# Two interleaved layers of Hedgehog attention and a squared-ReLU MLP: turned blocks' transfers tied behind the weight loads, and low parts of turned features on GpSimd

## The chip, the cores and the metric

The kernel runs on one core of one Trainium2 chip. The metric is the device time of one execution in microseconds (us). The engines are TensorE (PE; its weight loads are listed as PEld), VectorE (DVE), ScalarE (ACT), GpSimd (POOL) and SyncE (SP), which issues nearly all DMAs here.

## The reference

Two layers; in each, an attention with a learned feature map is added to x, then an MLP with squared ReLU. S = 2048 rows, D = 576, H = 32 heads of 18, F = 4608, all fp32.

```python
def attention(x):                       # of a layer-normed x
    q, k, v = split_heads(x @ wqkv)
    pq, pk = q @ w_phi, k @ w_phi       # per head, 18x18
    phi_q = concat(softmax(pq), softmax(-pq))
    phi_k = concat(softmax(pk), softmax(-pk))
    kv, z = phi_k.T @ v, sum(phi_k)
    return (phi_q @ kv) / (phi_q @ z + 1e-6) @ wo
def mlp(x):
    return relu(x @ w1 + b1) ** 2 @ w2 + b2
for layer in range(2):
    x = x + attention(layernorm(x))
    x = x + mlp(layernorm(x))
```

## The kernel before

**Tiles.** The 2048 rows are four blocks of 512, each four tiles of 128. fp32 operands are split into a high part, rounded to the matmul's format, and a low part that holds the rest; each product is three matmuls: high by high, high by low, low by high. ACT makes a high part (a copy), DVE or POOL the low part (a subtraction).

**Stages.** A layer has an attention block that nothing covers (t0, t1), and then four MLPs, one for each block, of which two run as a pair. The first two MLPs of each layer are woven with attention of other blocks: m_3 (layer 0) and m_1 (layer 1) with the output of block a_2 (a_0) and the queries and features of a_0 (a_3); m_2 and m_0 with the output of a_0 (a_3) and then all of a_1 (a_2). In the names of the order the layer stands first: `m0_2` is m_2 in layer 0, `a0_1` is a_1 in layer 0; the trace leaves it out.

**An MLP step.** There are 36 steps, each for 128 columns of F. Step f loads w1's and w2's parts (`r1`, `r2`, lines 1159 and 1161, on SP), splits them (`h1`, `s2`: ACT at lines 1167 to 1169, the low parts on DVE at 1171 and 1174 and on POOL at 1175), makes `ph` in 14 matmuls (L1190), applies relu on ACT (`hr`, L1197), makes the high part `hb` on ACT (L1198), squares on ACT (L1199) and leaves the low part to DVE (L1200), and adds to `acc` in 15 matmuls (L1217 and L1208). As a rule `ph` of step f+1 stands between `ph` and `acc` of step f, so that ACT and DVE have the time of 14 matmuls.

**The turned features.** `g_features` makes the features of a block's four tiles: exponentials, sums, factors, scale (L853 and its neighbours), then `turn`: DVE transposes blocks of 32x32 in place (L897), and SP writes the tile in four DMAs into a DRAM buffer `ft` (L900). `g_out` reads them back feature by row (`fetch`, L928) in five groups of 126 or 72 partitions: two fetches are asked for at its start, the others as the groups are used. For each half of a group ACT makes the high part `fh` (L941) and DVE the low part `fl` (L942), and PE multiplies them with the keys' sums (`pn`, L964, three matmuls for each of ten half groups). ACT and DVE split the result `pn` (L966 to L970), and it is multiplied with wo (`po`, L999), added to x, and normed. The group tiles share four buffers (tag E) with the exponentials; `fh` and `fl` share four (tag ft).

**What sets the order.** The program is written as Python generators. `weave(main, other, rate)` interleaves the steps of an MLP with those of attention by the costs that the steps yield; `pipeline` runs stages over tiles one behind the other, the costs being the numbers in its last argument. A list scheduler then fixes the order in which each engine's instructions stand, with its own estimates of their costs, and the order is static on the chip: an instruction that waits holds up all behind it on its engine. `tc.issue_after(ins)` ties what is traced inside it behind `ins`; `held` ties the steps of a generator behind the last instructions of the MLP's step that `dense` remembers; `traced_on(engine)` is the instruction that the program traced last for an engine. DMAs on SP wait at SP's head for what they read or overwrite, so that a load behind a transfer waits for that transfer's source.

Of the kernel before, what the change touches and what calls it, by code (L numbers as in the profile page):

```python
# [13 lines left out]
P = 128  # L14
TB = 512
NT = TB // P
# [5 lines left out]
def layers_kernel(  # L22
# [96 lines left out]
    def pipeline(n, stages, costs):  # L119

        for i in range(n + len(stages) - 1):
            for k in reversed(range(len(stages))):
                if 0 <= i - k < n:
                    stages[k](i - k)
                    yield costs[k]
# [9 lines left out]
    def traced_on(engine):  # L135
        return next(i for i in reversed(nc.cur_bb.bb.instructions) if i.engine == engine.engine)
# [519 lines left out]
    def soft_exp(e):  # L656
        return nc.scalar.activation(e, e, AF.Exp)
# [148 lines left out]
    def held(gen, keys=("last",)):  # L806

        while True:
            with ExitStack() as behind:
                for key in keys:  # L810
                    behind.enter_context(tc.issue_after(dense[key].ins))
                cost = next(gen, gen)
            if cost is gen:
                return
            yield cost
# [63 lines left out]
    def g_features(layer, raws, ph, name):  # L879

        rs, ms = {}, {}

        def start(t):
            ph.append(soft_parts(raws[t], f"{name}Q{t}"))

        def add(t):
            rs[t] = soft_sums(ph[t], f"{name}Q{t}")
            ms[t] = phi_products(layer, ph[t], f"{name}m{t}")

        def factors(t):  # L890
            phi_factors(phi_sums(ms.pop(t), f"{name}u{t}"), rs[t])

        turned[name] = home = dram.tile([2 * D, TB], F32, name=f"{name}ft")

        def turn(t):
            flat = ph[t].rearrange("p s d -> p (s d)")
            nc.vector.transpose(flat, flat)  # L897
            for i in range(NQ):
                at = t * P + 32 * i
                nc.sync.dma_start(home[:, at : at + 32].rearrange("(j f) r -> f j r", f=32),  # L900
                                  flat[32 * i : 32 * i + 32].rearrange("f (j r) -> f j r", r=32))

        yield from held(pipeline(NT, (start, lambda t: soft_exp(ph[t]), add, factors, lambda t: phi_scale(ph[t], rs[t]),
                                      turn), (2.6, 0.4, 3.0, 2.8, 1.2, 1.6)), ("last", "squared"))

    def g_out(layer, b, ph, dst, name, parts=1, pause=None, behind=None, norm=None, mid=None, costs=(None, None), o_first=None):

# [14 lines left out]
        def fetch(k):  # L922
            if k < NG:
                g, w = groups[k], gw[groups[k]]
                raws[g] = sb.tile([P, 2 * D], F32, tag="E", name=f"{name}w{g}", bufs=4)[:w, : 2 * TB]
                raws[g] = raws[g].rearrange("p (s n) -> p s n", s=2)
                src = turned[name].rearrange("(s d) n -> d s n", s=2)
                nc.sync.dma_start(raws[g], src[g * GW : g * GW + w])  # L928

        def turn(part, i):  # L930
            g, s = groups[i // 2], i % 2
            w = gw[g]
            new = lambda k: sb.tile([GW, TB], F32R, tag="ft", name=f"{name}f{k}{g}{s}{part}", bufs=4)[:w]
            if parts > 1:
                f = new("")
                fh, fl = (f[:, k * pw : (k + 1) * pw] for k in range(2))
            else:
                if s == 0:
                    fetch(i // 2 + 2)
                fh, fl = (new(k) for k in "hl")  # L940
                dense["turn", i] = nc.scalar.activation(fh, raws[g][:, s], AF.Copy)  # L941
                dense["turned"] = nc.vector.tensor_sub(fl, raws[g][:, s], fh.bitcast(F32))  # L942
                return fh, fl
            pt = wtile(f"{name}pt{g}{s}{part}")
            for t in range(NT // parts):
                nc.tensor.transpose(pt[:w, t * P : (t + 1) * P],
                                    ph[part * NT // parts + t][:, s, g * GW : g * GW + w], ident)
            dense["turn", i] = nc.scalar.activation(fh, pt[:w, :pw], AF.Copy)
            dense["turned"] = nc.vector.tensor_sub(fl, pt[:w, :pw], fh.bitcast(F32))
            return fh, fl  # L950
# [62 lines left out]
        if parts == 1:  # L1013
            for k in range(2):
                fetch(k)
        xs_of = []
        if pause:
            product, total, factors, rescale = pause
# [681 lines left out]
    def g_attend(layer, b, x, raws, dst, name, behind=None, norm=None, mid=(None, None), ph=None):  # L1700

        if ph is None:
            ph = []
            if raws is None:
                raws = []
                yield from g_queries(layer, b, x, raws, name)
            yield from g_features(layer, raws, ph, name)
        yield 5.0
        if mid[0]:
            yield from mid[0]  # L1710
        yield from g_out(layer, b, ph, dst, name, behind=behind and (behind["last"],), norm=norm, mid=mid[1],
                         costs=(1.0, None if norm else 3.0))
# [272 lines left out]
```

## Time and profile before

| what | us |
|---|---|
| median of 3 runs | 2442.39 |
| lowest and highest | 2441.28, 2443.29 |
| the profiled execution | 2441.59 |
| its span, first to last instruction | 2439.9 |
| PE busy in it | 2410.0 |
| DVE, ACT, POOL busy | 1560.5, 1289.7, 940.6 |
| mean clock granted to PE | 0.998 |

The span is the time from the first to the last instruction; 1.7 us of the execution lie around it. Busy time is the time in which an engine worked on something. PE's idle time is what is left of the span, 29.9 us. A row of the waits names the line that stood still and the line that it waited for. A row of the timeline gives start, length, engine, line, result and operands, and in brackets the engine's idle time just before with what ended it. A row of windows gives, for a stretch from:to, its length, the busy time of PE, PEld, DVE, ACT and POOL, then PE's granted clock, the DMA share and GB/s.

### The profile page before, as it was taken

To read this page: it belongs to the slowest core of one execution; us is meant where nothing else is said; L and a number is where in the kernel's file an instruction comes from. 1 tells how busy PE (TensorE), PEld (TensorE's weight loads), DVE (VectorE), ACT (ScalarE), POOL (GpSimd) and SP (SyncE) were. 2 spreads that over 40 slices of the span, in tenths; PEclk is the share of its full clock that TensorE was granted. 3 is DMA by queue.
4 is the path that set the end of the run, shared out by engine and by line. 5 is a ranking of instruction groups with operands and counts; after the bars stand their busy time and mean duration, and the time that the engine had idled before them with its cause. 6 is when DMAs were issued, how large, how long until landed. Compare 5 with 4: busy or idle time off the path is not lost. (4 is left out here: it accounts for less than half of the span.)

```text
span 2439.9 us, 41475 instructions
## 1 busy us (share of the span) xinstructions
PE 2410.0 (99%) x14806; PEld 2137.9 (88%) x14806; DVE 1560.5 (64%) x2537; ACT 1289.7 (53%) x2543; POOL 940.6 (39%) x1121
## 2 busy tenths in 40 slices
PE   9999999999999999999999999999999999999999
PEld 8999888888888888888999988888887888888898
DVE  8779847664867655545766787486557675555443
ACT  4344555444456666664443444554455466676643
POOL 4555303212335565542433442032222455565321
PEclk9999999999999999999999999999999999999999
DMA  9124573666654533338753156537667444333364
GB/s 338 64 84 165 163 194 97 151 202 220 155 173 136 157 99 115 109 104 302 257 188 139 59 173 143 168 96 186 191 233 158 141 142 145 118 103 116 110 199 130
DMA packets 370646, 379.40 MB, mean 155 GB/s; under 512 B 142886, under 2 KB 270790, under 8 KB 367878
## 3 DMA queue, kind: packets, MB, share of 16 engines
q1 hardware_dynamic: 369180, 375.37, 51.2%
q8 instruction: 116, 1.90, 0.3%
q10 hardware_dynamic: 1258, 1.37, 0.2%
q14 instruction: 92, 0.75, 0.1%
HBM read 297.22 MB, written 79.41 MB: 154 GB/s over the span
## 5 line engine op out<-in xcount | busy, mean ns | idle before, releaser
L1507 POOL TENSOR_TENSOR m_ps<-m_pr,m_ps 128x128 fp32r<-128x128 f32 x144 | 98.6, 685 | 337.8 <-ACT m_ps L1505 310.7
L1506 DVE TENSOR_TENSOR m_ps<-m_pr,m_ps 128x448 fp32r<-128x448 f32 x144 | 99.8, 693 | 175.9 <-ACT m_ps L1504 175.8
L1549 PE MATMUL m_pacc<-m_ps,m_phb 128*128 128x448 f32 x864 | 185.6, 363 | 0.0
L1549 PEld LDWEIGHTS m_pacc<-m_ps,m_phb 128*128 128x128 f32 x864 | 161.9, 188 | 15.0
L1549 PE MATMUL m_pacacc<-m_ps,m_phc 128*128 128x448 f32 x648 | 147.1, 365 | 0.0
L1504 ACT ACTIVATE m_ps<-m_pr 128x448 fp32r<-128x448 f32 x144 | 82.8, 575 | 115.7 <-issue 64.9
L1549 PEld LDWEIGHTS m_pacacc<-m_ps,m_phc 128*128 128x128 f32 x648 | 119.2, 188 | 7.7
L1190 PE MATMUL m_0ph<-a_0nh,m_0h 128*128 128x512 f32 (+1 forms) x380 | 96.7, 382 | 1.6 <-ACT m_0hr L1197 1.4
L1190 PE MATMUL m_1ph<-t1onh,m_1h 128*128 128x512 f32 (+1 forms) x380 | 96.2, 381 | 2.0 <-ACT m_1hr L1197 1.8
L1217 PE MATMUL m_2acc<-m_2s,m_2hb 128*128 128x448 f32 x432 | 95.2, 367 | 2.9 <-ACT m_2s L1168 2.6
L1190 PE MATMUL m_3ph<-t0onh,m_3h 128*128 128x512 f32 (+1 forms) x380 | 96.1, 381 | 1.8 <-ACT m_3hr L1197 1.6
L1217 PE MATMUL m_0acc<-m_0s,m_0hb 128*128 128x448 f32 x432 | 95.0, 367 | 2.9 <-ACT m_0s L1168 2.6
L1190 PE MATMUL m_2ph<-a_2nh,m_2h 128*128 128x512 f32 (+1 forms) x380 | 96.6, 382 | 0.8 <-ACT m_2hr L1197 0.6
L1217 PE MATMUL m_3acc<-m_3s,m_3hb 128*128 128x448 f32 x432 | 94.2, 364 | 2.0 <-ACT m_3hb L1198 1.4
L1217 PE MATMUL m_1acc<-m_1s,m_1hb 128*128 128x448 f32 x432 | 94.2, 364 | 2.0 <-ACT m_1hb L1198 1.4
L1217 PEld LDWEIGHTS m_2acc<-m_2s,m_2hb 128*128 128x128 f32 x432 | 81.8, 190 | 11.7 <-ACT m_2s L1168 3.0
L1217 PEld LDWEIGHTS m_0acc<-m_0s,m_0hb 128*128 128x128 f32 x432 | 81.5, 190 | 11.7 <-ACT m_0s L1168 3.0
L1217 PEld LDWEIGHTS m_3acc<-m_3s,m_3hb 128*128 128x128 f32 x432 | 80.4, 188 | 10.6 <-ACT m_3hb L1198 2.1
L1217 PEld LDWEIGHTS m_1acc<-m_1s,m_1hb 128*128 128x128 f32 x432 | 80.4, 188 | 10.5 <-ACT m_1hb L1198 2.1
L1175 POOL TENSOR_TENSOR m_3s<-m_3r,m_3s 128x128 fp32r<-128x128 f32 x36 | 22.9, 637 | 161.9 <-ACT m_3s L1169 153.3
L1175 POOL TENSOR_TENSOR m_1s<-m_1r,m_1s 128x128 fp32r<-128x128 f32 x36 | 22.8, 635 | 162.0 <-ACT m_1s L1169 151.8
L1190 PEld LDWEIGHTS m_1ph<-t1onh,m_1h 128*128 128x128 f32 x380 | 68.8, 188 | 17.4 <-ACT m_1hr L1197 3.0
(2464 smaller groups left out, 7237.0 us busy)
## 6 DMA issues: line engine op xcount, KB each, us to landing
m_pr<-in_B_w SPq DMA_DIRECT2D x144, 288.0 KB
m_pr<-in_B_w SPq DMA_DIRECT2D x72, 256.0 KB
hd<-m_pu SPq DMA_DIRECT2D x72, 256.0 KB
m_pg<-hd SPq DMA_DIRECT2D x72, 256.0 KB
m_3r<-in_B_w SPq DMA_DIRECT2D x36, 288.0 KB
m_2r<-in_B_w SPq DMA_DIRECT2D x36, 288.0 KB
m_1r<-in_B_w SPq DMA_DIRECT2D x36, 288.0 KB
m_0r<-in_B_w SPq DMA_DIRECT2D x36, 288.0 KB
```

Source lines behind the costliest of these rows:

```text
L1175: nc.gpsimd.tensor_sub(s2[:, FC + P : FC + 2 * P], r2[:, R:], s2[:, FC : FC + P].bitcast(F32))
L1190: dense["hidden"] = nc.tensor.matmul(ph[:, cols], a, m, start=(k == 0), stop=(k == len(ops) - 1))
L1217: nc.tensor.matmul(acc[t][:, :R], a[:, rows], m, start=(f == 0 and k == 0), stop=(f == NF - 1 and k == 2))
L1504: nc.scalar.activation(s2[:, RO : RO + R], r2[:, :R], AF.Copy)
L1506: nc.vector.tensor_sub(s2[:, RO + R : RO + 2 * R], r2[:, :R], s2[:, RO : RO + R].bitcast(F32))
L1507: nc.gpsimd.tensor_sub(s2[:, FC + P : FC + 2 * P], r2[:, R:], s2[:, FC : FC + P].bitcast(F32))
L1549: nc.tensor.matmul(accs[b][t][:, :R], a[:, rows], m, start=(g == 0 and k == 0), stop=(g == NF - 1 and k == 2))
```

## The change

Four things change. `turn` only transposes; the four DMAs of a tile become a stage of their own, `store`, one place further on in the pipeline, tied behind the SP instruction traced last, which as a rule is the load of weights that the MLP asked for last. The last tile's store comes after another 4.0 of cost. The fetches of the turned features are tied in the same way, with a pause of 2.0 behind the first two. The low part `fl` is made by POOL and not by DVE, ten for each block's output, 60 in all, and is no longer remembered in `dense["turned"]`. Last, the pause between features and output is 2.0 and not 5.0.

```diff
@@ -895,13 +895,23 @@
         def turn(t):
             flat = ph[t].rearrange("p s d -> p (s d)")
             nc.vector.transpose(flat, flat)
-            for i in range(NQ):
-                at = t * P + 32 * i
-                nc.sync.dma_start(home[:, at : at + 32].rearrange("(j f) r -> f j r", f=32),
-                                  flat[32 * i : 32 * i + 32].rearrange("f (j r) -> f j r", r=32))
-
-        yield from held(pipeline(NT, (start, lambda t: soft_exp(ph[t]), add, factors, lambda t: phi_scale(ph[t], rs[t]),
-                                      turn), (2.6, 0.4, 3.0, 2.8, 1.2, 1.6)), ("last", "squared"))
+
+        def store(t):
+            flat = ph[t].rearrange("p s d -> p (s d)")
+            with tc.issue_after(traced_on(nc.sync)):
+                for i in range(NQ):
+                    at = t * P + 32 * i
+                    nc.sync.dma_start(home[:, at : at + 32].rearrange("(j f) r -> f j r", f=32),
+                                      flat[32 * i : 32 * i + 32].rearrange("f (j r) -> f j r", r=32))
+
+        def steps():
+            yield from pipeline(NT, (start, lambda t: soft_exp(ph[t]), add, factors, lambda t: phi_scale(ph[t], rs[t]),
+                                     turn, lambda t: t < NT - 1 and store(t)), (2.6, 0.4, 3.0, 2.8, 1.2, 1.2, 0.1))
+            yield 4.0
+            store(NT - 1)
+            yield 0.1
+
+        yield from held(steps(), ("last", "squared"))
@@ -925,7 +935,8 @@
-                nc.sync.dma_start(raws[g], src[g * GW : g * GW + w])
+                with tc.issue_after(traced_on(nc.sync)):
+                    nc.sync.dma_start(raws[g], src[g * GW : g * GW + w])
@@ -939,7 +950,7 @@
                 dense["turn", i] = nc.scalar.activation(fh, raws[g][:, s], AF.Copy)
-                dense["turned"] = nc.vector.tensor_sub(fl, raws[g][:, s], fh.bitcast(F32))
+                nc.gpsimd.tensor_sub(fl, raws[g][:, s], fh.bitcast(F32))
                 return fh, fl
@@ -1013,6 +1024,7 @@
             for k in range(2):
                 fetch(k)
+            yield 2.0
         xs_of = []
@@ -1705,7 +1717,7 @@
             yield from g_features(layer, raws, ph, name)
-        yield 5.0
+        yield 2.0
         if mid[0]:
```

Lines behind the first edit move by 4, those of the MLP step by 12: `ph` is L1202 after the change, `hr` L1209, `acc` L1229 and L1220, `fh` L952, `fl` L953, `pn` L975, the stores L904, the fetches L939.

In layer 0's m_2, SP's order around the loads of steps 17 and 18 was this before (`Q0e` to `Q3e` are the four tiles of block 1 being turned):

```order
L1161 DMA m0_2r2_16_7411<-in_B_w2 128x576
L1159 DMA m0_2r1_18_7536<-in_B_w1 128x4x128
L244 DMA m0_2r1_18_7536<-in_B_w1 64x128 x2
L900 DMA a0_1ft_7030<-a0_1Q0e_7031 32x36x32 x4
L900 DMA a0_1ft_7030<-a0_1Q1e_7088 32x36x32 x4
L1161 DMA m0_2r2_17_7473<-in_B_w2 128x576
L900 DMA a0_1ft_7030<-a0_1Q2e_7152 32x36x32 x4
L1161 DMA m0_2r2_18_7537<-in_B_w2 128x576
L900 DMA a0_1ft_7030<-a0_1Q3e_7273 32x36x32 x4
```

After the change it is this:

```order
L1173 DMA m0_2r2_16_7414<-in_B_w2 128x576
L904 DMA a0_1ft_7030<-a0_1Q0e_7031 32x36x32 x4
L1173 DMA m0_2r2_17_7471<-in_B_w2 128x576
L904 DMA a0_1ft_7030<-a0_1Q1e_7038 32x36x32 x4
L1171 DMA m0_2r1_18_7534<-in_B_w1 128x4x128
L244 DMA m0_2r1_18_7534<-in_B_w1 64x128 x2
L1173 DMA m0_2r2_18_7535<-in_B_w2 128x576
L904 DMA a0_1ft_7030<-a0_1Q2e_7152 32x36x32 x4
```

The load of w2 for step 17 has moved ahead of the second tile, that of w1 for step 18 has moved behind the first two.

On ACT, the same place before, from relu of step 17 on (`h1` and `s2` are splits of weights):

```order
L1197 ACTIVATE m0_2hr17_7565<-m0_2ph17_7486,b1t_190 128x512
L1198 ACTIVATE m0_2hb17_7566<-m0_2hr17_7565 128x512
L1199 ACTIVATE m0_2hr17_7565<-m0_2hr17_7565 128x512
L1197 ACTIVATE m0_2hr18_7622<-m0_2ph18_7550,b1t_190 128x512
L1198 ACTIVATE m0_2hb18_7623<-m0_2hr18_7622 128x512
L1199 ACTIVATE m0_2hr18_7622<-m0_2hr18_7622 128x512
L1168 ACTIVATE m0_2s2_17_7479<-m0_2r2_17_7473 128x448
```

And after, where the split of step 17 stands ahead of the first of these rows:

```order
L1209 ACTIVATE m0_2hr17_7563<-m0_2ph17_7484,b1t_190 128x512
L1210 ACTIVATE m0_2hb17_7564<-m0_2hr17_7563 128x512
L1211 ACTIVATE m0_2hr17_7563<-m0_2hr17_7563 128x512
L1179 ACTIVATE m0_2h1_18_7540<-m0_2r1_18_7534 128x640
L1180 ACTIVATE m0_2s2_18_7541<-m0_2r2_18_7535 128x448
L1181 ACTIVATE m0_2s2_18_7541<-m0_2r2_18_7535 128x128
L1209 ACTIVATE m0_2hr18_7618<-m0_2ph18_7548,b1t_190 128x512
```

The splits of steps 17 and 18 have moved ahead of the relu of step 18.

On PE, around `ph` of step 18, before:

```order
L1208 MATMUL m0_2acc4_6118<-m0_2hb16_7502,m0_2s2_16_7417 128x512 x3
L1190 MATMUL m0_2ph18_7550<-a0_2nh_5750,m0_2h1_18_7542 128x512 x5
L1190 MATMUL m0_2ph18_7550<-a0_2nl_5751,m0_2h1_18_7542 128x512 x4
L1190 MATMUL m0_2ph18_7550<-a0_2nh_5750,m0_2h1_18_7542 128x512 x5
L1217 MATMUL m0_2acc0_6114<-m0_2s2_17_7479,m0_2hb17_7566 128x448 x2
```

After the change:

```order
L1220 MATMUL m0_2acc4_6118<-m0_2hb17_7564,m0_2s2_17_7477 128x512 x3
L1202 MATMUL m0_2ph18_7548<-a0_2nh_5800,m0_2h1_18_7540 128x512 x5
L1202 MATMUL m0_2ph18_7548<-a0_2nl_5801,m0_2h1_18_7540 128x512 x4
L1202 MATMUL m0_2ph18_7548<-a0_2nh_5800,m0_2h1_18_7540 128x512 x5
L1229 MATMUL m0_2acc0_6114<-m0_2s2_18_7541,m0_2hb18_7619 128x448 x2
```

The `acc` of step 17 now stands ahead of `ph` of step 18, and `acc` of step 18 directly behind it; the same holds for step 19.

On POOL, at the start of the same MLP, before (`nd` is the rstd of block 2's norm, `x2` and `x3` its sums with the bias, `s2` the weights' parts):

```order
L1051 TENSOR_TENSOR a0_2x2_5754<-a0_2x2_5754,b2t_191 128x576
L463 TENSOR_SCALAR a0_2nd3_5899<-a0_2nm3_5898 128x1
L464 TENSOR_TENSOR a0_2nd3_5899<-a0_2nd3_5899,mhalf_188 128x1
L1175 TENSOR_TENSOR m0_2s2_0_6063<-m0_2r2_0_6057,m0_2s2_0_6063 128x128
L1051 TENSOR_TENSOR a0_2x3_5863<-a0_2x3_5863,b2t_191 128x576
L1175 TENSOR_TENSOR m0_2s2_1_6092<-m0_2r2_1_6086,m0_2s2_1_6092 128x128
L1175 TENSOR_TENSOR m0_2s2_2_6221<-m0_2r2_2_6215,m0_2s2_2_6221 128x128
```

After the change:

```order
L953 TENSOR_TENSOR a0_0fl010_6188<-a0_0w0_6177,a0_0fh010_6187 126x512
L1063 TENSOR_TENSOR a0_2x2_5854<-a0_2x2_5854,b2t_191 128x576
L1187 TENSOR_TENSOR m0_2s2_0_6063<-m0_2r2_0_6057,m0_2s2_0_6063 128x128
L463 TENSOR_SCALAR a0_2nd3_5984<-a0_2nm3_5983 128x1
L464 TENSOR_TENSOR a0_2nd3_5984<-a0_2nd3_5984,mhalf_188 128x1
L1063 TENSOR_TENSOR a0_2x3_5948<-a0_2x3_5948,b2t_191 128x576
L1187 TENSOR_TENSOR m0_2s2_1_6092<-m0_2r2_1_6086,m0_2s2_1_6092 128x128
L953 TENSOR_TENSOR a0_0fl400_6198<-a0_0w4_6179,a0_0fh400_6197 72x512
L1187 TENSOR_TENSOR m0_2s2_2_6234<-m0_2r2_2_6228,m0_2s2_2_6234 128x128
L953 TENSOR_TENSOR a0_0fl410_6207<-a0_0w4_6179,a0_0fh410_6206 72x512
L953 TENSOR_TENSOR a0_0fl100_6217<-a0_0w1_6181,a0_0fh100_6216 126x512
L953 TENSOR_TENSOR a0_0fl110_6293<-a0_0w1_6181,a0_0fh110_6292 126x512
```

The low parts have moved in between the norm's small operations and the parts of the weights. PE's products with them stand closer together there than before:

```order
L975 MATMUL a0_0pn40_6210<-a0_0fh400_6197,kbh0_2812 128x512
L975 MATMUL a0_0pn40_6210<-a0_0fh400_6197,kbl0_2813 128x512
L975 MATMUL a0_0pn40_6210<-a0_0fl400_6198,kbh0_2812 128x512
L1202 MATMUL m0_2ph2_6241<-a0_2nh_5800,m0_2h1_2_6233 128x512 x3
L975 MATMUL a0_0pn40_6210<-a0_0fh410_6206,kbh0_2812 128x512
```

Before, one matmul of `ph` stood between the second and the third of these, and the rest of `ph` of step 2 with an `acc` behind the third.

## The prediction

> **What bounds the kernel now.** I read the head of the page first, then the waits of TensorE (PE), then the timeline at the longest of them.
>
> ```profile
> span 2439.9 us, 41475 instructions
> PE 2410.0 (99%) x14806; PEld 2137.9 (88%) x14806; DVE 1560.5 (64%) x2537; ACT 1289.7 (53%) x2543; POOL 940.6 (39%) x1121
> PE   9999999999999999999999999999999999999999
> ```
>
> PE is busy for 2410.0 of 2439.9 us, so its own work sets the time, and the change does not touch the number of its matmuls. Only 29.9 us of idle PE and what a lowered clock costs are there to win or to add to. VectorE (DVE) at 64% and GpSimd (POOL) at 39% matter only where PE waits for them. Where it waits is listed by the line that waited and the line it waited for, with the total, the count and the longest in us:
>
> ```profile
> PE m_2acc L1217 <- ACT m_2s L1168: 2.6, 1, 2.6
> PE m_0acc L1217 <- ACT m_0s L1168: 2.6, 1, 2.6
> PE m_1ph L1190 <- ACT m_1hr L1197: 1.8, 3, 0.8
> PE m_3ph L1190 <- ACT m_3hr L1197: 1.6, 2, 0.8
> PE m_3acc L1217 <- ACT m_3hb L1198: 1.4, 1, 1.4
> PE m_1acc L1217 <- ACT m_1hb L1198: 1.4, 1, 1.4
> PE m_0ph L1190 <- ACT m_0hr L1197: 1.4, 1, 1.4
> PE a_2pn L964 <- ACT a_2fh L941: 1.1, 1, 1.1
> PE m_2ph L1190 <- ACT m_2hr L1197: 0.6, 1, 0.6
> PE m_3acc L1217 <- DVE m_3s L1174: 0.6, 1, 0.6
> PE m_1acc L1217 <- DVE m_1s L1174: 0.6, 1, 0.6
> PE a_1pn L964 <- ACT a_1fh L941: 0.4, 1, 0.4
> ```
>
> All twelve lie in the four MLPs that are woven with attention. The largest, 2.6 us once in m_2 and once in m_0, looks like this in the timeline of layer 0 (start, length, then the idle time before it and who ended it):
>
> ```profile
> 656.94 0.69 ACT L1197 ACTIVATE m_2hr<-m_2ph,b1t 128x512 f32<-128x512 f32 x1 [4.27 <-PE m_2ph L1190]
> 658.32 0.63 ACT L1199 ACTIVATE m_2hr<-m_2hr 128x512 f32<-128x512 f32 x1
> 658.86 0.56 ACT L1168 ACTIVATE m_2s<-m_2r 128x448 fp32r<-128x448 f32 x1
> 659.47 0.49 PE L1217 MATMUL m_2acc<-m_2s,m_2hb 128*128 128x448 f32 x1 [2.57 <-ACT m_2s L1168]
> 660.26 3.22 PE L1217 MATMUL m_2acc<-m_2s,m_2hb 128*128 128x448 f32 x8 [0.30 <-DVE m_2s L1174]
> ```
>
> ScalarE (ACT) was free for 4.27 us and then split w2's weights of step 17 only behind three operations of step 18. PE stood for 2.57 us, and 0.30 more for the low part. The weights had been asked for late: the issues on SyncE show step 17's load (L1161) behind the four transfers of a turned block (L900).
>
> ```profile
> 649.43 2.33 SPq L900 DMA_DIRECT2D a_1ft<-a_1Q1e  x4
> 651.86 0.59 SPq L1161 DMA_DIRECT2D m_2r<-in_B_w  x1
> ```
>
> The stall costs more than its length. Two windows right behind it, one in each layer, hold a PE clock of half (the 0.50 behind the engines' busy times):
>
> ```profile
> 659.79:663.20 3.41, 3.11 (x9) 2.64 (x9) 1.04 (x2) 0.78 (x2) 1.43 (x2) 0.50 1.39 224
> 1868.10:1871.51 3.41, 3.41 (x10) 2.97 (x9) 0.63 (x1) 0.78 (x2) 0.70 (x1) 0.50 1.17 193
> ```
>
> 3.41 us at half the clock do the work of 1.7, so each of the two places loses 2.57 + 0.30 + 1.7 = 4.6 us. No other stall in the woven MLPs, up to 1.4 us long, is followed by such a window.
>
> **The change part by part.** The sum is made against the profiled execution, 2441.6 us (the span and 1.7 outside it), which lies 0.8 below the median of 2442.4.
>
> *The long stall goes.* In the new order the load of step 17 is issued between the first and second turned block, and step 17's split stands ahead of step 17's own three operations on ACT, not behind those of step 18. Both places lose their 4.6: −9.1 us.
>
> *The stalls among the `pn` products that ACT caused* (1.4 and 1.1 in m_0, 0.6 and 0.4 in m_2) go with the order that made them: −3.5. The fetches of the turned features now stand behind the loads asked for last, up to two issues of 0.6 us later; the first product that needs them stands later too, so this costs nothing unless a load ahead of them has to wait for its buffer.
>
> *New tight places.* In m_2 and m_0 steps 18 and 19 now have their second product (`acc`) directly behind the first (`ph`) of the same step, with no matmul between. The rows of m_3acc and m_1acc on ACT's `hb` price that at 1.4 each, since relu (0.69) and the high part (0.63) must both pass. Four of them: +5.6. In m_3 and m_1 there were one such place, two of `ph` behind `ph` at 0.8, and 0.6 for DVE, 3.6 us in all; now there are three of the first kind, one of the second and about 0.1: 5.1, so with m_1's 3.8 it is +1.5 and +1.3, +2.8. Nothing covers these: a row of the order without a matmul in between has none to give.
>
> *The low parts move from DVE to POOL*, 60 instructions of 126 or 72 partitions by 512. DVE's price is measured; POOL never runs this shape, so its price is bounded by neighbours (min/median/max in ns in the first row, the mean behind the bar in the others):
>
> ```profile
> L942 DVE TENSOR_TENSOR a_0fl<-a_0w,a_0fh x20: 678/684/904, 485.8 to 1573.6; 126x512 fp32r<-126x512 f32 x16, 72x512 fp32r<-72x512 f32 x4
> L1484 POOL TENSOR_TENSOR m_pr<-m_pr 128x384 f32<-128x384 f32 x36 | 39.1, 1087 | 1.4
> L1051 POOL TENSOR_TENSOR a_2x<-a_2x,b2t 128x576 f32<-128x576 f32 x8 | 12.5, 1559 | 7.4 <-DVE a_2ne L495 3.6 <-DVE a_2ne L1292 2.9 <-PE m_0ph L1190 1.0
> L1171 POOL TENSOR_TENSOR m_3h<-m_3r,m_3h 128x640 fp32r<-128x640 f32 x2 | 3.1, 1567 | 5.4 <-ACT m_3h L1167 5.4
> ```
>
> 512 elements lie between 384 (1.09) and 576 or 640 (1.56): I take 1.3 us, from the line between 1.09 and the 640 row, which has the same output type. The bounds are 1.09 and 1.56. So 60 × 0.68 = 41 us leave DVE and 60 × 1.3 = 78 come onto POOL. Neither engine is full, so only the time from the high part to the third of each product's three matmuls counts. It grows by 1.3 − 0.68 = 0.6, and by what POOL has queued ahead. The place where most products stand close together is the start of m_2 (and of m_0), with block 0's (3's) output:
>
> ```profile
> 513.03 0.39 PE L964 MATMUL a_0pn<-a_0fh,kbl 126*126 126x512 f32 x1
> 513.26 0.40 PE L964 MATMUL a_0pn<-a_0fl,kbh 126*126 126x512 f32 x1
> 513.53 0.62 ACT L941 ACTIVATE a_0fh<-a_0w 72x512 fp32r<-72x512 f32 x1
> 514.47 0.73 POOL L1175 TENSOR_TENSOR m_2s<-m_2r,m_2s 128x128 fp32r<-128x128 f32 x1 [11.75 <-PE a_0pn L964]
> 514.53 0.40 PE L964 MATMUL a_0pn<-a_0fh,kbl 72*128 72x512 f32 x1
> ```
>
> These matmuls start 0.23 apart. The high part of group 4 ends at 513.53 + 0.62 = 514.15, so POOL's low part ends at 515.45; the new order has its matmul directly behind the one of 514.53, due at 514.76: 0.7 lost. Next on POOL come step 2's 128x128 part (0.73) and the second low part: 515.45 + 0.73 + 1.3 = 517.5. PE has six matmuls until then, 6 × 0.23 = 1.4, and comes at 516.85: 0.65 lost. Three more pairs (groups 2 and 3) stand as close, 0.3 to 0.4 each by the same reckoning: 1.0. Together 2.4 for each layer, 1.2 at a POOL step of 1.09, 3.3 at 1.56. What is behind these steps on POOL (the rstd of block 2's norm, the x2 addition, later weights' parts) has a microsecond and more to spare, POOL having idled 11.75 us here. The late groups of `pn` in m_2 and m_0 stand further apart (0.6 each, 0.2 to 1.1), those in m_3 and m_1 further still (0.2). Sum: 4.8 + 1.2 + 0.4 = +6.4, from +3 to +9.
>
> [...]
>
> *DVE around the transposes.* Taking `acc` of step 17 forward by one `ph` asks its low parts 3.2 us earlier. DVE is nearly full there:
>
> ```profile
> 1855.00:1863.80 8.80, 8.80 (x41) 7.21 (x39) 8.56 (x15) 1.96 (x3) 1.17 (x1) 1.00 0.64 119
> ```
>
> DVE is busy for 8.56 of 8.80 us (third pair), and none of its relief falls here: the low parts that go come later. With the rows of DVE's operations added up in the new order, the low part of step 17's weights ends 0.2 to 2.0 us late if every transpose stays put, and not at all if the scheduler's moves of them help. I take 0.5 for each layer: +1.0, from 0 to +4.
>
> **Sum:** −9.1 − 3.5 + 5.6 + 2.8 + 6.4 + 1.0 = +3.2 us, so 2444.8 for a profiled execution and 2445.6 for the median. 0.2% is 4.9 us, about what a measurement of this kernel can tell from no change; the bounds are 2437.5 and 2447.3. I forecast no change within it: the stalls that are removed come back as smaller ones.
>
> **The rivals.**
>
> *GpSimd keeps up: faster.* If POOL's low parts end before they are wanted (its step near 1.09, and ACT makes the high parts earlier than in the trace) and DVE is in time, 6.4 and 1.0 drop out: −4.2 against the median. There are also about five stalls fewer, and the matmul behind a stall is itself slow (0.49 us in the row above for the first `acc`), some 0.2 each: −5.2 in all, 2437.2. For it speaks POOL's 39% of busy time; against it the 0.23 us between matmuls that want a new low part every third one, a pace of 0.7 where POOL does 1.3.
>
> *GpSimd's steps block DVE: slower.* One DVE instruction of 64 elements stretched from 0.23 to 1.50 us beside a POOL product of 1.43 that started just before it:
>
> ```profile
> 653.61 0.23 DVE L848 TENSOR_TENSOR a_1Q3r<-a_1Q3r,a_1u 128x64 f32<-128x64 f32 x1
> 1824.99 1.43 POOL L835 TENSOR_TENSOR a_2m<-a_2Q1e,zb 128x576 f32<-128x576 f32 x1
> 1825.00 1.50 DVE L848 TENSOR_TENSOR a_2Q0r<-a_2Q0r,a_2u 128x64 f32<-128x64 f32 x1
> ```
>
> The 60 new steps run while DVE makes the low parts of the weights and of `hb`, both from operands in SBUF, and PE waits for these. A block costs up to 1.50 − 0.23 = 1.3. Four of the sixty on the path of PE give 5.1 on top of the forecast, 2450.7; from two on it is slower than the bound (2448.2). Against it: DVE then has 41 us less to do, and most of the steps meet a DVE that has time. [...]
>
> *The weights still come late: slower.* Step 17's load remains behind the first turned block on SyncE, which waits for DVE's transpose. If that is late, the 9.1 stay lost while the new places are paid: 2445.6 + 9.1 = 2454.7.
>
> **Chances.** The forecast 0.53 (0.40 within the bounds, 0.13 slower, as its own terms spread by 3 to 4 us), GpSimd keeping up 0.25 (2437.2 is at the bound: 0.20 faster, 0.05 within), blocking 0.17 (0.16 slower, 0.01 within), late weights 0.05 (slower). That makes faster 0.20, same 0.46, slower 0.34. The range is 2435 to 2451: it takes in the terms' own bounds, the centre of the fast rival and that of the blocking one, and leaves out about 0.08 below and 0.12 above.
>
> **What would show it.** Right: no wait of m_2acc or m_0acc on ACT's split above 1 us and no window at half clock; four new waits of `acc` on `hb` of 1.4; waits of `pn` on POOL of 0.3 to 0.9, some 6 us in all; DVE's busy time 41 us lower, POOL's 70 to 85 higher. Wrong: a POOL step under 1.15 us with hardly a wait on POOL (the fast rival), low parts on DVE of over 1 us with PE behind them (blocking), a half-clock window or a wait of 2 us on ACT's split (late weights).

## The result and the profile after

The changed kernel takes 2471.8 us (median; 2470.0 to 2476.0), the kernel before 2442.3 in the same comparison. The ratio is 1.0123, with a 95% interval from 1.0106 to 1.0141: 29.5 us slower, outside the range that was given.

The head of the page of the changed kernel:

```profile
span 2470.9 us, 41527 instructions
PE 2421.2 (98%) x14806; PEld 2137.6 (87%) x14806; DVE 1526.7 (62%) x2477; ACT 1292.4 (52%) x2543; POOL 1024.8 (41%) x1181
```

The span is 31.0 us longer. PE's idle time went from 29.9 to 49.7, so 19.8 are new waits; the other 11.2 are in PE's busy time (2410.0 to 2421.2, with the same 14806 matmuls), which means slower matmuls. DVE lost 34 us of work and POOL gained 84, near the 41 and 78 that were worked out. Apart from the loads that both kernels wait for at their start, PE's longest waits show what came and what went:

```profile
PE m_3acc L1229 <- ACT m_3hb L1210: 4.3, 3, 1.4
PE m_1acc L1229 <- ACT m_1hb L1210: 4.3, 3, 1.4
PE a_2pn L975 <- POOL a_2fl L953: 3.6, 7, 0.6
PE a_0pn L975 <- ACT a_0fh L952: 3.4, 2, 1.9
PE a_0pn L975 <- POOL a_0fl L953: 3.2, 5, 0.9
PE m_0acc L1229 <- ACT m_0hb L1210: 2.9, 2, 1.4
PE m_2acc L1229 <- ACT m_2hb L1210: 2.9, 2, 1.4
PE a_1pn L975 <- POOL a_1fl L953: 2.1, 4, 0.6
PE n_3p L512 <- DVE n_3n L490: 1.9, 1, 1.9
PE a_3pn L975 <- POOL a_3fl L953: 1.5, 2, 0.9
PE a_3pn L975 <- ACT a_3fh L952: 1.3, 1, 1.3
PE a_0po L1010 <- DVE a_0nh L534: 1.1, 1, 1.1
```

The two waits of 2.6 on ACT's split of step 17 are gone, as forecast. The waits of `acc` on `hb` are there in the number and length that the order gave: three in m_3 and m_1, two in m_2 and m_0, 1.4 each. New and not forecast are the three waits on ACT's `fh`, 4.7 us in all, and two on DVE, 1.9 in a norm (0.4 before) and 1.1 ahead of a `po`. The waits on POOL add up to 10.4 in 18 places.

Each of the three waits on `fh` (1.59, 1.85 and 1.29 us) is followed by half the clock, for 3.41, 6.82 and 3.40 us. In the timeline of m_2 (PE, with the idle time ahead in brackets) and in the windows behind the three places:

```profile
531.30 0.50 PE L975 MATMUL a_0pn<-a_0fh,kbh 126*126 126x512 f32 x1 [1.59 <-ACT a_0fh L952]
531.63 0.39 PE L975 MATMUL a_0pn<-a_0fh,kbl 126*126 126x512 f32 x1
532.93 0.50 PE L975 MATMUL a_0pn<-a_0fl,kbh 126*126 126x512 f32 x1 [0.91 <-POOL a_0fl L953]
```

```profile
533.40:536.81 3.41, 3.41 (x10) 2.62 (x9) 0.65 (x1) 1.25 (x3) 2.04 (x3) 0.50 0.99 325
1577.88:1584.70 6.82, 6.70 (x17) 5.17 (x16) 2.87 (x3) 3.04 (x6) 5.69 (x5) 0.50 0.99 228
1758.79:1762.19 3.40, 2.89 (x7) 2.33 (x8) 0.05 (x1) 0.63 (x1) 2.92 (x3) 0.50 0.87 268
```

13.6 us at half the clock, where before had 6.8: 3.4 us more lost in the profiled execution. The share differs between executions: the mean clock was 0.996 in the longest of the four (2476.0 us) and 0.999 in the shortest (2470.0).

Two causes of the waits on `fh` can be read from the queues. In m_1, SyncE's issues of the wo loads (L427) and of the first fetches (L939), and the first use on ACT:

```profile
1544.64 0.52 SPq L1173 DMA_DIRECT2D m_1r<-in_B_w  x1
1558.76 0.77 SPq L427 DMA_DIRECT2D a_0o0h<-wsoh  x2
...
1561.70 0.83 SPq L427 DMA_DIRECT2D a_0o1l<-wsol  x2
1563.48 0.80 SPq L939 DMA_DIRECT2D a_0w<-a_0ft  x2
```

```profile
1575.20 1.15 ACT L952 ACTIVATE a_0fh<-a_0w 126x512 fp32r<-126x512 f32 x2 [3.42 <-DMA a_0w<-a_0ft]
```

SyncE stood from 1545.2 to 1558.8 at the head of eight loads of wo. The fetch, now tied behind the last of them, was issued at 1563.5 and its data used at 1575.2, 11.7 us later; that the eight loads' transfers held it up is read from its place behind them, and e8_fetchfirst tests the place. Before, the fetch was issued at 1532.1, ahead of those loads. In m_2 (and m_0) the other cause: w1's part of step 4 lands late, and ACT holds `fh` of group 2 behind its split.

```profile
529.32 0.74 ACT L1179 ACTIVATE m_2h<-m_2r 128x640 fp32r<-128x640 f32 x1 [2.29 <-DMA m_2r<-in_B_w]
```

Its load was issued from 518.2 on, behind the same eight loads of wo for this block; before, from 509.7 on.

### The profile page after: what moved, and what is told of

Same layout as the page of the kernel before. It is cut to its first block, busy times and chain, and to the rows that moved or that the text cites. A ratio compares the mean times of both kernels' runs of the same rounds, so it can differ in the third digit from the quotient of the medians.

```text
span 2470.9 us, 41527 instructions
## 1 busy us (share of the span) xinstructions
PE 2421.2 (98%) x14806; PEld 2137.6 (87%) x14806; DVE 1526.7 (62%) x2477; ACT 1292.4 (52%) x2543; POOL 1024.8 (41%) x1181
## 4 chain that ended last, share of the span: by engine, by line
PE 83%; DVE 6%; issue 4%; DMA 3%; POOL 2%; ACT 2%; SPq 0%; POOLq 0%; DVEq 0%; ACTq 0%
PE m_ppx L1529 9%; PE m_pacc L1561 7%; PE m_pacacc L1561 5%; PE m_3ph L1202 4%; PE m_ppy L1529 4%; PE m_1ph L1202 4%; PE m_3acc L1229 3%; PE m_0ph L1202 3%; PE m_1acc L1229 3%; PE m_2ph L1202 3%; PE m_0acc L1229 2%; PE m_ppz L1529 2%; PE m_2acc L1229 2%; PE m_pacc L1551 2%; PE m_pacacc L1551 2%
## 5 line engine op out<-in xcount | busy, mean ns | idle before, releaser
L1229 PE MATMUL m_1acc<-m_1s,m_1hb 128*128 128x448 f32 x432 | 95.7, 367 | 4.3 <-ACT m_1hb L1210 4.3
L1229 PE MATMUL m_3acc<-m_3s,m_3hb 128*128 128x448 f32 x432 | 94.8, 365 | 4.3 <-ACT m_3hb L1210 4.3
L1229 PE MATMUL m_0acc<-m_0s,m_0hb 128*128 128x448 f32 x432 | 94.6, 364 | 3.9 <-ACT m_0hb L1210 2.9
L1229 PE MATMUL m_2acc<-m_2s,m_2hb 128*128 128x448 f32 x432 | 94.6, 364 | 3.9 <-ACT m_2hb L1210 2.9
L1202 PE MATMUL m_1ph<-t1onh,m_1h 128*128 128x512 f32 (+1 forms) x380 | 96.8, 385 | 1.3 <-ACT m_1hr L1209 1.0
L1202 PE MATMUL m_2ph<-a_2nh,m_2h 128*128 128x512 f32 (+1 forms) x380 | 97.1, 383 | 0.1
L1202 PE MATMUL m_0ph<-a_0nh,m_0h 128*128 128x512 f32 (+1 forms) x380 | 97.2, 383 | 0.0
L1202 PE MATMUL m_3ph<-t0onh,m_3h 128*128 128x512 f32 (+1 forms) x380 | 95.7, 381 | 1.0 <-ACT m_3hr L1209 0.8
L1229 PEld LDWEIGHTS m_1acc<-m_1s,m_1hb 128*128 128x128 f32 x432 | 81.1, 189 | 13.7 <-ACT m_1hb L1210 5.8
L1229 PEld LDWEIGHTS m_2acc<-m_2s,m_2hb 128*128 128x128 f32 x432 | 80.3, 188 | 13.8 <-ACT m_2hb L1210 4.4
L1229 PEld LDWEIGHTS m_0acc<-m_0s,m_0hb 128*128 128x128 f32 x432 | 80.3, 188 | 13.8 <-ACT m_0hb L1210 4.4
L1229 PEld LDWEIGHTS m_3acc<-m_3s,m_3hb 128*128 128x128 f32 x432 | 80.4, 188 | 13.6 <-ACT m_3hb L1210 5.8
L1202 PEld LDWEIGHTS m_1ph<-t1onh,m_1h 128*128 128x128 f32 x380 | 69.3, 190 | 16.7 <-ACT m_1hr L1209 1.9
L1202 PEld LDWEIGHTS m_3ph<-t0onh,m_3h 128*128 128x128 f32 x380 | 68.6, 188 | 15.9 <-ACT m_3hr L1209 1.4
L1543 DVE TENSOR_TENSOR m_phb<-m_pz,m_phb 128x512 fp32r<-128x512 f32 x72 | 59.0, 820 | 33.5 <-ACT m_pz L1538 32.0
```

The lines of the kernel that those rows point to most:

```text
L1202: dense["hidden"] = nc.tensor.matmul(ph[:, cols], a, m, start=(k == 0), stop=(k == len(ops) - 1))
L1229: nc.tensor.matmul(acc[t][:, :R], a[:, rows], m, start=(f == 0 and k == 0), stop=(f == NF - 1 and k == 2))
L1543: dense["paired"] = nc.vector.tensor_sub(hl, r, hh.bitcast(F32))
```

## The experiments

The kernel before lay between 2440.4 and 2442.3 us in the comparisons, so differences below are the ratio's, times 2441. The theory to begin with (1): most of the loss is GpSimd's pace, the rest comes from what the ties and pauses did to the transfers' places. The rival (2): the order on SyncE makes the loss, the engine of the low parts does not matter.

**e1_pool: only the low parts move.**

```diff
-                dense["turned"] = nc.vector.tensor_sub(fl, raws[g][:, s], fh.bitcast(F32))
+                nc.gpsimd.tensor_sub(fl, raws[g][:, s], fh.bitcast(F32))
```

> The kernel before, with one edit: GpSimd makes the low parts of the turned features (60 instructions); transfers, fetches and pauses as before. Theory 1 (the products of the turned features are paced by a low part of 1.28 us on GpSimd, 15 us of waits and slowed matmuls in the changed kernel, most of it from this edit alone): 6 to 14 us slower than before, with 3 to 8 us of waits of pn on POOL. Theory 2 (the order of the transfers and loads on SyncE makes the loss, the engine of the low part hardly matters): within 3 us of before.

2455.2 us, ratio 1.0055 (1.0038 to 1.0072): 13.4 slower. PE's order hardly differs from before's, the 2.6 us stalls are still there (one of them without half the clock behind it in this trace), and 23 waits on POOL of 11.4 us are new:

```profile
PE a_2pn L964 <- POOL a_2fl L942: 3.9, 8, 0.9
PE a_0pn L964 <- POOL a_0fl L942: 3.5, 7, 0.6
PE m_2acc L1217 <- ACT m_2s L1168: 2.6, 1, 2.6
PE a_1pn L964 <- POOL a_1fl L942: 2.4, 5, 0.9
PE a_3pn L964 <- POOL a_3fl L942: 1.6, 3, 0.6
```

So this edit alone costs nearly half of the loss, and rival 2 falls as it stood.

**e5_nopool: the change without it.** The changed kernel with the line above put back.

> The changed kernel with one edit taken back: the low parts on VectorE again. Theory 1: 8 to 16 us faster than the changed kernel (2456 to 2464), the waits of pn on POOL gone, the wait on a_0fh in m_1 and the half-clock stretch behind it still there. Theory 2: within 4 us of the changed kernel (2468 to 2476).

2460.6, ratio 1.0078 (1.0063 to 1.0093): 11.0 less than the changed kernel, as theory 1 said. The wait of a_0 in m_1 is still there (2.35 us, at 1568.5), but the half-clock stretch that theory 1 had behind it is not in this trace. 19 us of loss stay, though, with 9.4 us of waits of `pn` on `fh`. Theory 1 is right on GpSimd and incomplete on the rest.

**e8_fetchfirst: the first fetches ahead of wo's loads** in the changed kernel:

```diff
-        pair = pieces() if behind else None
         if parts == 1:
             for k in range(2):
                 fetch(k)
+        pair = pieces() if behind else None
+        if parts == 1:
             yield 2.0
```

> The changed kernel with the first two fetches asked for ahead of the loads of wo, so that they are tied behind the weights of the MLP and not behind wo's last load. If the late fetch in m_1 (issued at 1563.5, behind eight loads of wo that wait for their buffer, used at 1575.2) costs the 1.85 us wait and the 6.8 us at half clock behind it, this is 5 to 7 us faster than the changed kernel (2465 to 2467). If the products would have waited for GpSimd's low parts anyway: under 2 us faster.

2464.6, ratio 1.0094 (1.0079 to 1.0109): 7.1 us less than the changed kernel, at the upper end of the first reading. The wait in m_1 is gone: the fetch is issued at 1543.7, and SyncE stands at wo's loads only behind it, until 1557.2. By the starts of the last matmuls of an MLP (`py`), m_1 took 11.6 us longer than before in the changed kernel and 5.0 here, while m_3, whose first fetch moved from 342.9 to 325.2, gained nothing (5.1 and 5.2). The late fetch in m_1 cost 7.

**e2_store: only the stores as a tied stage** on the kernel before (the diff's `turn`, `store` and `steps`, nothing else).

> The kernel before, with one edit: the transfers of the turned blocks as a stage of their own, tied behind the loads. Theory 1: 0 to 4 us faster or slower than before, the 2.57 us stalls of m_2 and m_0 and their half-clock stretches gone (9 us), given back by steps whose second product stands directly behind the first. Theory 2: 10 us or more slower than before.

2454.5, ratio 1.0054 (1.0039 to 1.0069): 13.2 slower, where theory 1 had 0 to 4. The long stalls of step 17 did go, but longer ones came at the start of m_2 and m_0:

```profile
PE a_0pn L974 <- ACT a_0fh L951: 6.0, 2, 4.9
PE a_3pn L974 <- ACT a_3fh L951: 4.2, 1, 4.2
```

```profile
531.60 0.74 ACT L1177 ACTIVATE m_2h<-m_2r 128x640 fp32r<-128x640 f32 x1 [5.58 <-DMA m_2r<-in_B_w]
```

It is the place in m_2 that was seen in the changed kernel, worse. A new theory: the stage's costs make attention fall behind. The turn and the transfers of a block now yield 4 × 1.2 + 4 × 0.1 + 4.0 + 0.1 = 9.3 where they yielded 4 × 1.6 = 6.4. Of the features, only a_2's own stand ahead of its products in m_3 (its last tile is turned at 309.1, those of a_0 from 432 on). At 3.7 of cost for each MLP step of 6.3 us, 2.9 more is an estimated 4.9 us; the first `pn` of a_2 starts at 353.5, not 345.2, so 8.3 us later, and the reckoning covers part of it. The last of wo's eight loads in m_2 then follows at 519.1, not 508.9, and the MLP's weights behind it.

**e10_store_pause: the same with nearly the total of costs as before** (6.5, where before had 6.4).

```diff
-            yield 4.0
+            yield 1.2
             store(NT - 1)
```

> As e2_store (transfers as a tied stage for every attention, 2454.5 us), but with 1.2 instead of 4.0 ahead of the last tile's transfer, so that a block's features yield the same total of costs as before. Theory 1 (the larger total makes attention lag: the products of a_2 begin 8 us later in m_3, the buffer of wo comes free later, the loads of wo and behind them w1's part of step 4 are late, and PE waits 4.9 and 4.2 us at the start of m_2 and m_0): these two waits and the half-clock stretches behind them go, 2438 to 2444. Theory 2 (the tie itself delays the loads): the waits stay, 2452 to 2456.

2440.0, ratio 0.9999 (0.9990 to 1.0008): one number, the pause, was worth 13.4 us, and what is left of the edit, the tie, changes nothing in the sum. The first `pn` of a_2 is back at 346.2, and the waits on `fh` at the start of m_2 and m_0 are gone. That is only half of the gain, though: by the starts of `py` the two profiled executions differ by 4.4 us in m_2 and 3.7 in m_0, but also by 4.9 in m_3 and 4.1 in m_1, where one wait of `acc` on `hb` less (1.4) shows a part. But m_2 and m_0 wait again in their middle, on the split of w1:

```profile
PE m_2ph L1200 <- ACT m_2h L1177: 2.8, 1, 2.8
PE m_0ph L1200 <- ACT m_0h L1177: 2.6, 1, 2.6
```

The last tile's four transfers are again ahead of that load on SyncE, and ACT waits 5.80 for it:

```profile
659.60 2.32 SPq L904 DMA_DIRECT2D a_1ft<-a_1Q3e  x4
661.96 0.65 SPq L1169 DMA_DIRECT2D m_2r<-in_B_w  x1
666.53 0.74 ACT L1177 ACTIVATE m_2h<-m_2r 128x640 fp32r<-128x640 f32 x1 [5.80 <-DMA m_2r<-in_B_w]
```

**e9_tied_last: tied, with the pause, only where it helps**, in the features of a_1 (layer 0) and a_2 (layer 1), which fall into m_2 and m_0.

```diff
+        tied = name in ("a0_1", "a1_2")
...
+            if not tied:
+                yield from pipeline(NT, stages, (2.6, 0.4, 3.0, 2.8, 1.2, 1.6))
+                return
```

> The kernel before, with the transfers as a stage of their own and tied only for the last attention of each layer (a_1 in layer 0, a_2 in layer 1), whose features fall into m_2 and m_0. Theory 1 (the tie itself is worth the 9 us of the long stalls; what the transfers edit loses is lost in m_3, m_1 and at the start of m_2 and m_0, where attention lags behind): the long stalls and their half-clock stretches gone, two new waits of acc on hb of 1.4, 7 to 11 us faster than before (2430 to 2434). Theory 2 (the tie as such slows the loads): slower than before.

2434.3, ratio 0.9976 (0.9966 to 0.9986): 5.9 us faster than before, and the best version here. No window at half clock is left inside the span, and the two new waits that were expected, one in each of m_2 and m_0, are there:

```profile
PE m_0acc L1237 <- ACT m_0hb L1218: 1.4, 1, 1.4
...
PE m_2acc L1237 <- ACT m_2hb L1218: 1.4, 1, 1.4
```

The last tile's transfers now stand behind the load that they stood ahead of in e10_store_pause:

```profile
658.21 0.64 SPq L1179 DMA_DIRECT2D m_2r<-in_B_w  x1
660.81 3.69 SPq L907 DMA_DIRECT2D a_1ft<-a_1Q3e  x4
```

The gain is a little under the 7 to 11 expected.

**e16_tied_last_pause: the same with 1.2 for 4.0.**

> As e9_tied_last (2434.3 us), with 1.2 instead of 4.0 ahead of the last tile's transfer. If attention's lag costs in m_2 and m_0 too: 1 to 4 us faster than e9_tied_last (2430 to 2433). If the pause is what keeps the transfers clear of the weights there: 2 us or more slower, with a long stall back in m_2 or m_0.

2439.7, ratio 0.9993 (0.9984 to 1.0002): 4.2 us of e9_tied_last's gain lost, with a long wait back in each of the two:

```profile
PE m_2ph L1210 <- ACT m_2h L1187: 2.2, 1, 2.2
PE m_0ph L1210 <- ACT m_0h L1187: 2.1, 1, 2.1
```

So the pause of 4.0 helps in the second attention, where it keeps the last transfer clear of the weights, and harms in the first, where it delays everything behind it.

**e11_after_pause: e8_fetchfirst with 1.2 for 4.0.**

> As e8_fetchfirst (the changed kernel with the first fetches ahead of wo's loads, 2464.6 us), and with 1.2 instead of 4.0 ahead of the last tile's transfer. If the lag is a cause of its own beside GpSimd's low parts: the waits of pn on ACT behind a late h1 at the start of m_2 and m_0 and their half-clock stretches go, 8 to 10 us less, 2454 to 2457. If GpSimd's low parts would have held these products up anyway: 2461 to 2465.

2461.9, ratio 1.0084 (1.0071 to 1.0098): 2.4 less than e8_fetchfirst by the ratios, which the intervals don't tell from nothing, and inside the case of 2461 to 2465. The waits on `fh` at the start of m_2 and m_0 did go, though, as the first case had it. Others came in their place: 2.4 and 1.5 of the norm's products `np` on VectorE (none above 0.2 in e8_fetchfirst) and 1.7 on `fh` of a_1. So the lag's 13 us of e2_store and GpSimd's loss do not add up; why the other waits came is open.

**e12_all_but_pool: e11_after_pause with the low parts on VectorE.**

> As e11_after_pause (2461.9 us), with the low parts on VectorE again: all of the change but GpSimd, with the fetches ahead of wo's loads and 1.2 ahead of the last transfer. Theory 1 (GpSimd's pace is the largest single loss, and what else the change lost came from the lag and from fetches behind wo): 2438 to 2446. Rival (the tied order itself costs 10 us or more in the steps): 2450 to 2456.

2446.2, ratio 1.0025 (1.0015 to 1.0034), at the upper end of theory 1's 2438 to 2446: 6.1 slower than before. GpSimd's price here, the difference to e11_after_pause, is 14.4. What stays is mostly the order in m_3 and m_1, 3.4 us each by the starts of their last matmuls (`py`); m_2 and m_0 together come out ahead.

```profile
PE m_3acc L1230 <- ACT m_3hb L1211: 3.3, 3, 1.4
```

**e3_fetch: only the fetches tied, with the pause of 2.0 behind the first two**, on the kernel before.

> The kernel before, with one edit: the fetches tied behind the last instruction on SyncE, and the pause of 2.0 behind the first two. By the place found in the changed kernel (the first fetch of a_0 in m_1 stands behind eight loads of wo that wait for their buffer): 4 to 8 us slower than before, with one wait of a_0pn on ACT of about 2 us in m_1 and a half-clock stretch behind it. If the fetch is hidden when the low parts are on VectorE: within 2 us.

2472.8, ratio 1.0134 (1.0120 to 1.0148): 32.7 slower, as much alone as the whole change, where 4 to 8 were expected. The products of a_0, a_2 and a_3 wait on `fh` (7.4, 2.8 and 3.9 us), and in the profiled execution (2478.5 us) the clock is halved in five places for 27.3 us, 13.7 of loss:

```profile
PE a_0pn L965 <- ACT a_0fh L942: 7.4, 2, 4.1
```

**e13_fetch_ahead: the same with the fetches ahead of wo's loads** (the edit of e8_fetchfirst).

> As e3_fetch (fetches tied and the pause of 2.0 behind them, alone: 2472.8 us), with the first two fetches ahead of wo's loads. If the 32 us of e3_fetch come from fetches that stand behind wo's loads in m_3 and m_1, and from half the clock behind the waits: 2440 to 2450, no wait of pn on ACT above 1 us in m_3 and m_1. If they come from the tie or the pause itself: above 2460.

2466.3, ratio 1.0103 (1.0088 to 1.0118): the second case. The place behind wo is worth 7.6 here as it was 7.1 in the changed kernel, no wait of `pn` on `fh` above 1 us is left in m_3 and m_1, and 25 us stay. They lie in m_2 (9 us) and m_0 (7), where a load of w1 again lands late, and in m_3 and m_1 (4 each). Whether the tie or its pause of 2.0 makes them wasn't separated. e12_all_but_pool has both as well and is 6.1 slower; there the pause between features and output is 2.0 and not 5.0, so that the two pauses together are 1.0 shorter than before and not 2.0 longer. That speaks against the tie and for the shift, without showing it.

**e6_nofetch: the changed kernel with the fetches as before.**

> The changed kernel with the fetches as before (no tie, no pause of 2.0 behind them). In its order the first fetch in m_3 and m_1 still stands behind wo's loads, because the last tile is stored late. Theory 1: it keeps GpSimd's loss and the late fetch, 2463 to 2472. Rival (the tie of the fetches is the loss): 2445 to 2455.

2466.7, ratio 1.0103 (1.0087 to 1.0118): within theory 1's 2463 to 2472. Without the tie the fetch in m_1 is still issued behind wo's loads in the order that results.

**e4_yield: only the 2.0 for 5.0** between features and output, on the kernel before.

> The kernel before, with one edit: 2.0 and not 5.0 between features and output. Theory 1 (only attention's lag matters, and this makes it smaller): within 5 us of before, no new wait above 2 us. Rival (any shift of the weave costs as much as the transfers did): 8 us or more slower.

2453.4, ratio 1.0049 (1.0034 to 1.0064): 12.0 slower. The rival of this run was right: attention that is earlier costs as much here as the lag did in e2_store. In the profiled execution 10.1 us of 14.3 lie in m_2. a_2's first `pn` comes 6.5 us sooner, and at the start of m_2 w2's split, with `fh` behind it, waits for a load:

```profile
515.65 0.58 ACT L1168 ACTIVATE m_2s<-m_2r 128x448 fp32r<-128x448 f32 x1 [3.78 <-DMA m_2r<-in_B_w]
```

So the lag theory holds only in part. What e2_store, e4_yield and e13_fetch_ahead share is one place: at the start of m_2 and m_0 the loads of wo, the stores of x and the MLP's weights stand in one queue, and a load of weights lands late in each. That the order which falls out of the costs decides who is late is the reading of this; and it is not the only place, as e2_store loses 10.6 of its 15 us in m_3 and m_1.

**e14_idle_pool: GpSimd's load without the wait.** On the kernel before, beside VectorE's low parts:

```diff
                 dense["turned"] = nc.vector.tensor_sub(fl, raws[g][:, s], fh.bitcast(F32))
+                nc.gpsimd.tensor_sub(raws[g][:, s], raws[g][:, s], raws[g][:, s])
```

> The kernel before, with VectorE making the low parts as before and GpSimd given 60 subtractions of the same shape besides, whose results nobody reads; the order of PE, ACT and VectorE is that of before. It leaves the price of GpSimd's load on its neighbours without the wait for its result. If the loss of e1_pool (14 us) is the pace at which GpSimd delivers: within 3 us of before. If it is VectorE being held up by GpSimd's reads (the rival of the prediction): 6 us or more slower, with instructions of VectorE of over 1.2 us ahead of waits of PE.

2445.5, ratio 1.0015 (1.0006 to 1.0024): 3.7 slower, between the two theories, 1.5 to 5.9 by the interval. So the smaller part of e1_pool's 13.4 is the burden on neighbours and the larger one, an estimated 10, the wait for the result. It is an estimate because the load isn't the same: here GpSimd starts when VectorE has read the group, writes it in place, and VectorE keeps its own 60. VectorE's busy time rose from 1560.5 to 1577.1 with no instruction more. How the burden acts can be seen in the changed kernel, where a VectorE instruction that started 0.06 after a low part took 1.51 us; the same operation without one took 0.55 in the kernel before.

```profile
498.13 1.29 POOL L953 TENSOR_TENSOR a_0fl<-a_0w,a_0fh 126x512 fp32r<-126x512 f32 x1
498.19 1.51 DVE L490 TENSOR_SCALAR a_2nn<-a_2x,a_2nm,a_2nd 128x512 f32<-128x512 f32 x1 [0.44 <-POOL a_2nd L464]
```

```profile
494.14 0.55 DVE L490 TENSOR_SCALAR a_2nn<-a_2x,a_2nm,a_2nd 128x512 f32<-128x512 f32 x1 [0.54 <-POOL a_2nd L464]
```

**e15_half_pool: GpSimd makes every second low part.**

```diff
+                low = nc.gpsimd.tensor_sub if s else nc.vector.tensor_sub
+                made = low(fl, raws[g][:, s], fh.bitcast(F32))
```

> As e1_pool (2455.2 us, 14 slower than before), but GpSimd makes only the second low part of each group, VectorE the first: 30 instructions. If pace is the cause, GpSimd then has 1.28 us for two products, 6 matmuls of 0.23, and mostly keeps up: a quarter or less of the loss, 2441 to 2445. If each instruction on GpSimd costs the same wherever it stands: half, 2447 to 2449.

2450.0, ratio 1.0039 (1.0027 to 1.0052): 9.5 slower (6.6 to 12.7) for 30 instructions, above both cases, and no quarter of 13.4 (9.3 to 17.6); the intervals leave room for a half. PE's waits on POOL are half of e1_pool's, 5.9 us in 11 places for 11.4 in 23. So the word pace was wrong: GpSimd did not fall behind a stream here, single low parts came too late for the matmul that stands behind them (0.5 us on average in both).

```profile
PE a_0pn L967 <- POOL a_0fl L943: 2.5, 4, 0.6
PE a_2pn L967 <- POOL a_2fl L943: 1.8, 4, 0.6
```

## Why the prediction was wrong

The loss, 30.0 us by the ratio of 1.0123, can be read along four kernels in a row, each with one edit less: 7.1 for the fetch behind wo's loads (to e8_fetchfirst), 2.4 for the pause ahead of the last transfer (to e11_after_pause), 14.4 for GpSimd (to e12_all_but_pool), and 6.1 for what is left, the new order. Against the forecast of +3.2, the low parts were put at 6.4 and cost 14.4; the late fetch and the pause ahead of the last transfer were put at nothing; and all other terms together were put at −3.2 and came to +6.1, with the pause taken out. The 2.4 is within the noise. In another sequence the shares differ: GpSimd costs 13.4 alone and 11.0 as the first edit taken back, the stores 13.2 alone, the fetches 32.7 alone, the shorter pause 12.0 alone. The four alone would give 71 us. They are not independent.

*The long stall goes: right.* No wait on step 17's split, and no half-clock window there. The smaller waits that were to go with it (3.5) went too.

*The new tight places: right to a tenth.* 2.9 each in m_2 and m_0 and 4.3 in m_3 and m_1 stand in the waits, where 2.8 and 4.2 were counted. But they are not all that the order costs: in e12_all_but_pool m_3 and m_1 lose 3.4 each where 1.5 and 1.3 were put, and the norm's products `np` wait 3.6 on VectorE, which the sum did not have. Why they are late there is open.

*The low parts on POOL: the step that failed in size.* The instruction was put at 1.3 us, and it took 1.29 (median of the first group, min and max beside it in ns), so its length was right:

```profile
L953 POOL TENSOR_TENSOR a_2fl<-a_2w,a_2fh x20: 1272/1287/1880, 352.9 to 1929.8; 126x512 fp32r<-126x512 f32 x16, 72x512 fp32r<-72x512 f32 x4
```

The failing sentence is "The late groups of `pn` in m_2 and m_0 stand further apart (0.6 each, 0.2 to 1.1), those in m_3 and m_1 further still (0.2). Sum: 4.8 + 1.2 + 0.4 = +6.4, from +3 to +9." In e1_pool, m_3 lost 2.8 and m_1 2.5 by the starts of their last matmuls, where 0.2 each was put, m_2 4.3 and m_0 5.1, where 3.0 each was put. Only the tightest place was worked out from the order, and the others got a word. What one wait costs was also left at its length: the first matmul behind each took 0.50 in the rows above where its neighbours took 0.39. And some 3.7 of it, by e14_idle_pool, is the burden on neighbours, which had been put into a rival and not into the sum.

*The fetches: a condition stated and not looked up.* "this costs nothing unless a load ahead of them has to wait for its buffer" was the whole of it. The order of the changed kernel has eight such loads ahead of the first fetch in m_1, and that SyncE would stand there was to be seen coming, if not for 13.6 us: in the trace of before it pauses from 1541.5 to 1546.3 ahead of the same loads. 7.1 us, half-clock windows included.

*A term that was missing.* Nothing in the sum stood for the costs that the steps yield, 6.4 to 9.3 for a block's turn and transfers, 2.0 new behind the first fetches and 5.0 to 2.0 between features and output, though they set how far attention stands from the MLP beside it. e2_store against e10_store_pause gives 13.4 us for one of these numbers, and e4_yield 12.0 for another.

*DVE around the transposes:* 1.0 was put down; the waits on DVE's low parts in the changed kernel are 0.7 and 0.3 in each layer, 2.0, inside its bounds.

The rival that ended slower had the direction. What it says of DVE was seen once more, in the 1.51 us beside a low part, and the load on GpSimd costs 3.7 us in e14_idle_pool, an interval (1.5 to 5.9) that takes in the 5.1 that the rival put on top; that all of it comes by way of DVE was not shown, and it was not what decided.

What stays open: in e3_fetch and e13_fetch_ahead, which of the tie and the pause of 2.0 makes the 25 us; which part of the new order makes the 6.1; and why m_2 and m_0 start without a long wait in before, e9_tied_last, e10_store_pause, e12_all_but_pool and e16_tied_last_pause and in no other order without GpSimd's part, beyond what the queue at that place shows.

## What to carry to other kernels

In a static order an instruction that is 0.6 us slower can cost its difference at every place where its consumer stands directly behind (23 of 60 in e1_pool, 11.4 us), however idle its engine is (41% busy in the changed kernel): count those places all through the program. A tie behind "the last instruction of a queue" is only as good as what that instruction is, so read the order for what waits at the head of the queue. And numbers that pace one stream against another are part of the change: compare the totals before and after, and tie only where the stall is (here 5.9 us faster than before instead of 29.5 slower).

## What the runs showed of the hardware

Half the clock did not need one long stall. In the changed kernel 1.59 and 0.91 us of idle PE, 2.50 in a stretch of 3.23 (529.70 to 532.93), were followed by 3.41 us at 0.50, while 1.44 alone never was in the profiles of the two kernels, nor 1.92 alone (in the changed kernel, up to 1139.5). Nor does a stall of one length always bring it: the wait of 2.57 in m_2 was followed by such a window in the kernel before and not in e1_pool, where the same wait stands. The reading of this is that it matters where the wait falls. The two half-clock windows behind the long stalls of the kernel before start 1208.31 us apart (659.79 and 1868.10), 354 times 3.413, and one lasts 3.41; those of the changed kernel start 1044.48 and 180.91 us apart (533.40, 1577.88, 1758.79), 306 and 53 times 3.413. Counted back in stretches of that length from a half-clock window of the same trace, the stall fills one stretch in before (first row: PE busy for 0.84 of 3.41) and is split over two in e1_pool (1.78 and 2.15):

```profile
656.38:659.79 3.41, 0.84 (x4) 0.28 (x2) 2.19 (x3) 2.62 (x5) 0.10 (x1) 1.00 1.22 184
660.24:663.65 3.41, 1.78 (x8) 1.13 (x6) 2.62 (x4) 1.53 (x3) 0.03 (x1) 1.00 0.90 149
663.65:667.06 3.41, 2.15 (x9) 1.77 (x10) 1.64 (x3) 1.86 (x5) 0.99 (x2) 1.00 1.22 220
```

No sharp limit comes out of it: in the changed kernel the stretches from 529.99, 1574.47 and 1755.37, with 1.20, 1.56 and 1.74 of busy PE, were followed by half the clock, and the one from 1137.56, with 1.49, was not. What lowers the clock was not shown beyond these rows.
